# Another distribution of a block's convolution over its sixteen steps

## The chip, the cores and the metric

The kernel runs on one core of a Trainium2 chip. The metric is device time in microseconds of one launch. Engines are named as in the profile: PE (matrix products; PEld are its weight loads), DVE or VectorE, ACT or ScalarE, POOL or GpSimd, SP (which issues the DMA transfers; SPq is its queue).

## The reference

A causal convolution over seven tokens with a softmaxed weight per head, then a two-layer network. All data are float32.

```python
# x: 8 x 4096 x 192, weight: 8 heads x 7 taps; 24 channels share a head
w = softmax(weight, axis=-1)
x_pad = concat([zeros(B, 6, D), x], axis=1)
out[b, s, c] = sum(w[head(c), k] * x_pad[b, s + k, c] for k in range(7))
x = out.reshape(32768, 192)
h = x @ w_in                       # 192 x 2048
g = where(h >= 1, h, where(h <= -1, 0, (h + 1) ** 2 / 4))
return g @ w_out                   # 2048 x 192
```

## The kernel before, in words

The 32768 tokens are 64 tiles of 512; two tiles, A and B, make a block, so there are 32 blocks. Hidden units go in eight pairs of 128, so a tile takes eight steps and a block sixteen. The loop at the end of the kernel runs over steps `q`; `i = q % 16` is the step in the block, and c the block. Steps 0 to 7 are the network on tile A, 8 to 15 on tile B.

To keep float32 precision, matrix operands are split in two parts, hi and lo, and three products are summed. In each step:

- PE runs `mm1(q)` (L422, 18 pairs of products into a PSUM tile `h`, of which there are two) and then `mm2(q - 2)` (L462, 20 into four accumulators: `accm0`, `accm1`, `accr0`, `accr1`), which takes `gh` and `gl` of two steps ago.
- VectorE clips `h` (L473), makes `gl` of the step before (L497, `g - gh`, both from SBUF), and takes the maximum (L484), which frees `h`.
- ScalarE makes `gh` of the step before (L491, a cast), then the square (L479).

After a tile's eighth `mm2`, in steps 1 and 9, ScalarE copies the four accumulators out (L509, four copies), so that the next `mm2` can start; POOL adds them (L511); in steps 2 and 10 follow a small copy (L521) and addition (L522), and VectorE's transposes for the store (L534).

Around this the convolution of the next tokens is done, in channel-major layout. A block has three units: `b` (tile B's first 128 channels, for this same block's steps 8 to 15), `a` (tile A's first 128, for the next block) and `r` (the remaining 64 channels of both tiles, for the next block). A unit goes through:

- "T": VectorE transposes the loaded tile `raw` into `xT` (L147). For `b` this is done at the end of step 15.
- tap 0: ScalarE writes `y = w * xT` (L226). Taps 1 to 6: ScalarE makes a product `p` (L219), POOL adds it to `y` (L230).
- "split": ScalarE casts `y` to hi (L248, for `r` L262); lo is `y - hi`, on POOL for `a` and `b` (L252), on VectorE for `r` (L263). SP issues four transfers that exchange the halves (L235, L236).

Buffers rotate: two each of `xT` and `y`, three of `p`, three of `raw`. All three loads of a block are issued in step 0. Each engine works its instructions in the order in which the program writes them; nothing reorders them. `conv_slot(i, ...)`, called at the end of a step's work on the engines but ahead of the store's part, looks up in three tables, `PLAN_B`, `PLAN_A` and `PLAN_R`, what each unit does in step `i`. Block 0 uses other tables for `a` and `r` (`FIRST_A`, `FIRST_R`).

```python
PLAN_B = {0: (0, 1), 2: (2, 3), 3: (4, 5), 4: (6,), 5: "split"}
PLAN_A = {4: ("T", 0), 5: (1, 2), 6: (3, 4), 7: (5, 6), 8: "split"}
PLAN_R = {7: ("T",), 8: (0, 1, 2), 10: (3, 4), 11: (5, 6), 13: "split"}
```

Of the kernel before, what the change touches and what calls it, by code (L numbers as in the profile page):

```python
# [30 lines left out]
def lightconv_then_ffn(ctx: ExitStack, tc: tile.TileContext, x, weight, w_in, w_out, out):  # L31
# [669 lines left out]

    PLAN_B = {0: (0, 1), 2: (2, 3), 3: (4, 5), 4: (6,), 5: "split"}
    PLAN_A = {4: ("T", 0), 5: (1, 2), 6: (3, 4), 7: (5, 6), 8: "split"}
    PLAN_R = {7: ("T",), 8: (0, 1, 2), 10: (3, 4), 11: (5, 6), 13: "split"}


    FIRST_B = {2: 2, 3: 3, 4: 4, 5: 5}
# [4 lines left out]
    def conv_slot(i, b, a, r):  # L714
        early = b.c == 0
        plans = ((None if early else b, PLAN_B), (a, FIRST_A if early else PLAN_A),
                 (r, FIRST_R if early else PLAN_R))
        for u, plan in plans:
# [201 lines left out]
```

## Time and profile before

| | |
|---|---|
| median of 3 runs | 2170.52 us (2169.75 to 2170.53) |
| profiled execution | 2170.33 us, span 2168.6 us |
| granted PE clock | 0.999 |
| busy | PE 2153.0, DVE 2084.0, ACT 1684.8, POOL 1139.4 us |
| L230, POOL, y + p | 546 x 1454 ns |
| L497, DVE, gl | 497 x 1478 ns |
| L484, DVE, max | 505 x 1215 ns |
| L473, DVE, clip | 505 x 1198 ns |
| L219, ACT, product p | 562 x 714 ns |

Busy shares are averages over the whole run and include the time in which an engine is held up within an instruction. To read where time is lost, follow the start times of the same instruction from step to step. In a row of the timeline the first number is the start in us from the span's start, the second the duration; x6 means six instructions merged in one row, and what stands in brackets is idle time ahead of it and what ended it.

### The profile page before, as it was taken

The numbers are of one execution on the slowest core, as the hardware profiler recorded it, in microseconds if no ns is written. First come the engines' busy times: TensorE is split into PE (matmuls) and PEld (weight loads), VectorE is DVE, ScalarE is ACT, GpSimd is POOL, SyncE is SP. The second block draws the span as 40 slices with busy tenths as digits, with TensorE's granted clock in tenths as the row PEclk, the third lists the DMA queues.
The fourth block names the chain that finished last, engine by engine and source line by source line (L and its number), as shares of the span: only waits on it lengthen the run. The fifth ranks groups of instructions, "written<-read, shape, count | busy, mean of one in ns | idle before, by whom it ended". The sixth has DMA issues, their size and how long they took to land.

```text
span 2168.6 us, 48144 instructions
## 1 busy us (share of the span) xinstructions
PE 2153.0 (99%) x19646; PEld 1875.8 (86%) x19646; DVE 2084.0 (96%) x1883; ACT 1684.8 (78%) x2153; POOL 1139.4 (53%) x868
## 2 busy tenths in 40 slices
PE   9999999999999999999999999999999999999999
PEld 6998888888888888888888888888888888998887
DVE  8899999999999999999999999999999999999998
ACT  7778877778777788777887787877878777788775
POOL 1556644566445565555654456644556545565451
PEclk9999999999999999999999999999999999999999
DMA  6222222222222222222122222222222222212211
GB/s 165 51 53 42 46 50 51 53 51 42 51 48 50 55 41 53 51 48 55 37 51 51 51 53 48 44 49 48 53 55 40 53 51 47 56 35 53 51 35 25
DMA packets 439197, 110.83 MB, mean 51 GB/s; under 512 B 407360, under 2 KB 414912, under 8 KB 438976
## 3 DMA queue, kind: packets, MB, share of 16 engines
q1 hardware_dynamic: 438816, 107.65, 25.9%
q8 instruction: 155, 2.54, 0.5%
q14 instruction: 66, 0.54, 0.1%
q10 hardware_dynamic: 160, 0.10, 0.0%
HBM read 32.84 MB, written 25.17 MB: 27 GB/s over the span
## 4 chain that ended last, share of the span: by engine, by line
DVE 27%; PE 24%; ACT 19%; POOL 13%; issue 13%; SPq 3%; DMA 1%; POOLq 0%; DVEq 0%; ACTq 0%
POOL y L230 11%; PE h L422 10%; DVE g L484 9%; DVE g L473 8%; PE accm L462 7%; DVE gl L497 7%; ACT g L479 6%; ACT gh L491 5%; PE accr L462 4%; ACT t L509 4%; DVE osb L534 2%; SPq L95 2%; ACT p L219 2%; POOL lo L252 2%; DMA raw<-in_x_dram 1%
## 5 line engine op out<-in xcount | busy, mean ns | idle before, releaser
L230 POOL TENSOR_TENSOR y<-y,p 128x512 f32<-128x512 f32 x546 | 793.8, 1454 | 751.0 <-DVE g L484 541.5
L497 DVE TENSOR_TENSOR gl<-g,gh 128x1024 fp32r<-128x1024 f32 (+1 forms) x497 | 734.4, 1478 | 51.6 <-ACT gh L491 41.3
L491 ACT CAST gh<-g 128x1024 fp32r<-128x1024 f32 (+1 forms) x497 | 520.4, 1047 | 255.4 <-DVE g L484 244.1
L422 PE MATMUL h<-hi,w 64*128 64x512 f32 x4032 | 701.2, 377 | 0.0
L479 ACT ACTIVATE g<-g 128x1024 f32<-128x1024 f32 (+1 forms) x505 | 535.1, 1060 | 167.3 <-DVE g L473 157.0
L484 DVE TENSOR_TENSOR g<-h,g 128x1024 f32<-128x1024 f32 (+1 forms) x505 | 613.3, 1215 | 8.3 <-ACT g L479 4.4
L473 DVE TENSOR_SCALAR g<-h 128x1024 f32<-128x1024 f32 (+1 forms) x505 | 604.7, 1198 | 11.6 <-PE h L422 10.6
L462 PE MATMUL accm<-gh,w 64*128 64x512 f32 x3968 | 604.2, 378 | 9.3 <-ACT t L509 9.1
L422 PEld LDWEIGHTS h<-hi,w 64*128 64x128 f32 x4032 | 523.7, 186 | 47.9
L422 PE MATMUL h<-lo,w 64*128 64x512 f32 x2016 | 540.5, 376 | 0.0
L462 PEld LDWEIGHTS accm<-gh,w 64*128 64x128 f32 x3968 | 449.4, 186 | 77.0 <-ACT t L509 29.4
L462 PE MATMUL accm<-gl,w 64*128 64x512 f32 x1984 | 379.2, 381 | 0.0
L219 ACT ACTIVATE p<-xT,wk 128x512 f32<-128x512 f32 x562 | 376.2, 714 | 0.0
L462 PE MATMUL accr<-gh,wr 64*128 64x512 f32 x1984 | 373.4, 376 | 0.0
L462 PE MATMUL accr<-gl,wr 64*128 64x512 f32 x1984 | 373.4, 376 | 0.0
L422 PEld LDWEIGHTS h<-lo,w 64*128 64x128 f32 x2016 | 330.2, 186 | 24.6
L422 PE MATMUL h<-rh,w 64*128 64x512 f32 x992 | 293.5, 376 | 0.0
L422 PE MATMUL h<-rhi,w 64*128 64x512 f32 x992 | 293.5, 376 | 0.0
L462 PEld LDWEIGHTS accm<-gl,w 64*128 64x128 f32 x1984 | 250.9, 186 | 33.4 <-DVE gl L497 12.3
L462 PEld LDWEIGHTS accr<-gl,wr 64*128 64x128 f32 x1984 | 257.3, 186 | 24.8 <-DVE gl L497 0.2
L462 PEld LDWEIGHTS accr<-gh,wr 64*128 64x128 f32 x1984 | 257.3, 186 | 24.7 <-ACT gh L491 0.2
L422 PEld LDWEIGHTS h<-rhi,w 64*128 64x128 f32 x992 | 184.5, 186 | 14.9
(141 smaller groups left out, 1867.6 us busy)
## 6 DMA issues: line engine op xcount, KB each, us to landing
out_dram<-osb SPq DMA_DIRECT2D x366, 64.0 KB
raw<-in_x_dram SPq DMA_DIRECT2D x334, 68.0 KB
hi<-hi SPq DMA_DIRECT2D x126, 128.0 KB
lo<-lo SPq DMA_DIRECT2D x126, 128.0 KB
rhi<-rh SPq DMA_DIRECT2D x62, 128.0 KB
rlo<-rl SPq DMA_DIRECT2D x62, 128.0 KB
words<-in_moe_w_in_dram SPq DMA_DIRECT2D x16, 192.0 KB
words<-in_moe_w_out_dram SPq DMA_DIRECT2D x8, 384.0 KB
```

The costliest lines, as they stand in the source:

```text
L95: (engs[i] if engs else nc.sync).dma_start(out=raw[i * SQ:(i + 1) * SQ, lo:n // SQ + 1, :], in_=src.rearrange("(j a) b -> a j b", a=SQ),)
L219: nc.scalar.mul(p, self.xT[:, SH + k:SH + k + TB], wk[:, self.wsel, k:k + 1])
L230: nc.gpsimd.tensor_add(y, y, self.product(k))
L252: eng.tensor_sub(lo, self.y, hi.bitcast(F32))
L422: nc.tensor.matmul(to, w[HALVES[e], c0:c0 + P], of, start=(n == 0), stop=(n == len(mms) - 1))
L462: nc.tensor.matmul(both(accs[s][a, i]), st, turns(g[HALVES[i], e, :]), start=(j == 0 and n == first[a]), stop=(j == NPAIR - 1 and n == las ...
L473: nc.vector.tensor_scalar(out=g[:, e, :], in0=hs[q][:, e, :], scalar1=-1.0, scalar2=1.0, op0=ALU.max, op1=ALU.min)
L479: nc.scalar.activation(g[:, e, :], g[:, e, :], AF.Square, bias=0.5, scale=0.5)
L484: nc.vector.tensor_tensor(out=g[:, e, :], in0=h[:, e, :], in1=g[:, e, :], op=ALU.max)
L491: nc.scalar.copy(gh[:, e, :], gs[q][:, e, :])
L497: eng.tensor_sub(gl[:, e, :], g[:, e, :], gh[:, e, :])
L509: nc.scalar.copy(t[i][:, n], acc[a, i][:, n])
```

## The change

The three tables are changed; nothing else is.

```diff
-    PLAN_B = {0: (0, 1), 2: (2, 3), 3: (4, 5), 4: (6,), 5: "split"}
-    PLAN_A = {4: ("T", 0), 5: (1, 2), 6: (3, 4), 7: (5, 6), 8: "split"}
-    PLAN_R = {7: ("T",), 8: (0, 1, 2), 10: (3, 4), 11: (5, 6), 13: "split"}
+    PLAN_B = {0: (0, 1, 2), 2: (3, 4), 3: (5, 6), 5: "split"}
+    PLAN_A = {3: ("T", 0), 4: (1, 2), 5: (3, 4), 6: (5, 6), 11: "split"}
+    PLAN_R = {4: ("T",), 7: (0, 1), 8: (2, 3), 10: (4,), 11: (5,), 12: (6,), 13: "split"}
```

Tile B's taps are done by step 3 instead of 4, tile A's begin in step 3 instead of 4 and its split goes from step 8 to 11; the rest's transpose goes from step 7 to 4, and its taps, three, two and two at a time in steps 8, 10 and 11, become two, two, one, one and one in steps 7, 8, 10, 11 and 12.

The order on POOL, one block, before. The first row is the last two additions of the block ahead and this block's first; the two `lo` are B's split and A's.

```order
L230 TENSOR_TENSOR y<-y,p 128x512 x3
L511 TENSOR_TENSOR sum<-t 128x512 x2
L230 TENSOR_TENSOR y<-y,p 128x512 x2
L522 TENSOR_TENSOR sum<-sum,t 64x512
L230 TENSOR_TENSOR y<-y,p 128x512 x3
L252 TENSOR_TENSOR lo_7877<-y,hi_7876 128x512
L230 TENSOR_TENSOR y<-y,p 128x512 x6
L252 TENSOR_TENSOR lo_8049<-y,hi_8048 128x512
L230 TENSOR_TENSOR y<-y,p 128x512 x2
L511 TENSOR_TENSOR sum<-t 128x512 x2
```

The same block on POOL with the change. Here the first row is the last two additions of the block ahead and two of this one.

```order
L230 TENSOR_TENSOR y<-y,p 128x512 x4
L511 TENSOR_TENSOR sum<-t 128x512 x2
L230 TENSOR_TENSOR y<-y,p 128x512 x2
L522 TENSOR_TENSOR sum<-sum,t 64x512
L230 TENSOR_TENSOR y<-y,p 128x512 x4
L252 TENSOR_TENSOR lo_7886<-y,hi_7885 128x512
L230 TENSOR_TENSOR y<-y,p 128x512 x7
L511 TENSOR_TENSOR sum<-t 128x512 x2
L230 TENSOR_TENSOR y<-y,p 128x512
L522 TENSOR_TENSOR sum<-sum,t 64x512
L252 TENSOR_TENSOR lo_8228<-y,hi_8227 128x512
```

One more addition stands ahead of the first sums and one more ahead of B's split; A's `lo` goes behind the second sums (L511). Between the two `lo` stand seven additions, the sums, another addition and L522, where six additions stood.

VectorE, from step 2's gl to step 5's clip, before:

```order
L497 TENSOR_TENSOR gl<-g,gh 128x1024
L484 TENSOR_TENSOR g<-h,g 128x1024
L534 STREAM_TRANSPOSE osb<-sum 128x512
L473 TENSOR_SCALAR g<-h 128x1024
L497 TENSOR_TENSOR gl<-g,gh 128x1024
L484 TENSOR_TENSOR g<-h,g 128x1024
L534 STREAM_TRANSPOSE osb<-sum 64x512
L473 TENSOR_SCALAR g<-h 128x1024
L497 TENSOR_TENSOR gl<-g,gh 128x1024
L484 TENSOR_TENSOR g<-h,g 128x1024
L147 STREAM_TRANSPOSE xT<-raw 128x544
L473 TENSOR_SCALAR g<-h 128x1024
```

The same place with the change, from step 3's clip on:

```order
L473 TENSOR_SCALAR g<-h 128x1024
L497 TENSOR_TENSOR gl<-g,gh 128x1024
L484 TENSOR_TENSOR g<-h,g 128x1024
L147 STREAM_TRANSPOSE xT<-raw 128x544
L534 STREAM_TRANSPOSE osb<-sum 64x512
L473 TENSOR_SCALAR g<-h 128x1024
L497 TENSOR_TENSOR gl<-g,gh 128x1024
L484 TENSOR_TENSOR g<-h,g 128x1024
L147 STREAM_TRANSPOSE xT<-raw 128x544
L473 TENSOR_SCALAR g<-h 128x1024
```

Two unit transposes (A's and the rest's) now stand here instead of one, A's ahead of the store's transpose; the one in step 7 is gone.

ScalarE in steps 8 and 9, up to the copies of the accumulators, before:

```order
L479 ACTIVATE g<-g 128x1024
L248 CAST hi_7127<-y 128x512
L226 ACTIVATE y<-xT,wk 128x512
L219 ACTIVATE p<-xT,wk 128x512 x2
L491 CAST gh<-g 128x1024
L479 ACTIVATE g<-g 128x1024
L509 COPY t<-accm_6750 128x512
```

And with the change:

```order
L479 ACTIVATE g<-g 128x1024
L219 ACTIVATE p<-xT,wk 128x512 x2
L491 CAST gh<-g 128x1024
L479 ACTIVATE g<-g 128x1024
L509 COPY t<-accm_6753 128x512
```

The cast and the tap 0 are gone from between the two squares; two products are left.

## The prediction

> **What bounds the kernel now.** I read the page's busy shares first, then the list of waits, then the start of each step on PE, then VectorE, GpSimd and ScalarE row by row through one block, the fifteenth after the first. All blocks between the second and the last look alike to 0.1 us.
>
> ```profile
> PE 2153.0 (99%) x19646; PEld 1875.8 (86%) x19646; DVE 2084.0 (96%) x1883; ACT 1684.8 (78%) x2153; POOL 1139.4 (53%) x868
> ...
> PEld accm L462 <- ACT t L509: 29.4, 58, 0.7
> DVE gl L497 <- ACT gh L491: 41.3, 110, 0.6
> PEld accm L462 <- DVE gl L497: 12.3, 54, 0.3
> ```
>
> PE and DVE are both nearly full, so averages do not say which one sets the pace. PE waits in two places: for the accumulators to be copied out (58 waits, two in each of 29 blocks) and for gl. The starts of mm1 show where:
>
> ```profile
> 1021.41 0.80 PE L422 MATMUL h<-hi,w 64*128 64x512 f32 x4
> 1025.51 0.80 PE L422 MATMUL h<-hi,w 64*128 64x512 f32 x4
> ...
> 1046.01 0.80 PE L422 MATMUL h<-hi,w 64*128 64x512 f32 x4
> 1050.33 0.60 PE L422 MATMUL h<-hi,w 64*128 64x512 f32 x4
> ...
> 1058.54 0.59 PE L422 MATMUL h<-hi,w 64*128 64x512 f32 x4
> 1062.79 0.59 PE L422 MATMUL h<-hi,w 64*128 64x512 f32 x4
> 1067.75 0.80 PE L422 MATMUL h<-hi,w 64*128 64x512 f32 x4
> ...
> 1088.26 0.80 PE L422 MATMUL h<-hi,w 64*128 64x512 f32 x4
> ```
>
> These are steps 0, 1, 6, 7, 9, 10, 11 of one block and step 0 of the next. An undisturbed step is 4.10 us, sixteen are 65.62 (the five steps from 1025.51 to 1046.01 are 20.50). The block takes 66.85. The 1.23 us lie in step 6 (4.32 instead of 4.10), step 9 (4.25) and step 10 (4.96). If nothing held PE, 29 blocks would be 35.7 us shorter.
>
> **What makes PE wait** is the chain on VectorE. Per step it runs clip (L473), gl of the step before (L497), max (L484); max to max is the length of a step there.
>
> ```profile
> 1027.00 1.23 DVE L484 TENSOR_TENSOR g<-h,g 128x1024 f32<-128x1024 f32 x1
> ...
> 1029.39 1.31 DVE L497 TENSOR_TENSOR gl<-g,gh 128x1024 fp32r<-128x1024 f32 x1
> 1030.63 1.21 DVE L484 TENSOR_TENSOR g<-h,g 128x1024 f32<-128x1024 f32 x1
> ...
> 1035.09 1.21 DVE L484 TENSOR_TENSOR g<-h,g 128x1024 f32<-128x1024 f32 x1
> ...
> 1037.95 2.11 DVE L497 TENSOR_TENSOR gl<-g,gh 128x1024 fp32r<-128x1024 f32 x1
> 1039.99 1.21 DVE L484 TENSOR_TENSOR g<-h,g 128x1024 f32<-128x1024 f32 x1
> ...
> 1044.06 1.22 DVE L484 TENSOR_TENSOR g<-h,g 128x1024 f32<-128x1024 f32 x1
> 1045.20 0.73 DVE L147 STREAM_TRANSPOSE xT<-raw 128x544 f32<-128x544 f32 x1
> ...
> 1047.66 1.22 DVE L497 TENSOR_TENSOR gl<-g,gh 128x1024 fp32r<-128x1024 f32 x1 [0.62 <-ACT gh L491]
> 1048.80 1.22 DVE L484 TENSOR_TENSOR g<-h,g 128x1024 f32<-128x1024 f32 x1
> ...
> 1056.30 1.21 DVE L484 TENSOR_TENSOR g<-h,g 128x1024 f32<-128x1024 f32 x1
> ...
> 1059.20 2.13 DVE L497 TENSOR_TENSOR gl<-g,gh 128x1024 fp32r<-128x1024 f32 x1
> 1061.26 1.21 DVE L484 TENSOR_TENSOR g<-h,g 128x1024 f32<-128x1024 f32 x1
> ...
> 1064.86 1.22 DVE L484 TENSOR_TENSOR g<-h,g 128x1024 f32<-128x1024 f32 x1
> ...
> 1069.57 1.21 DVE L484 TENSOR_TENSOR g<-h,g 128x1024 f32<-128x1024 f32 x1
> ...
> 1074.39 1.21 DVE L484 TENSOR_TENSOR g<-h,g 128x1024 f32<-128x1024 f32 x1
> ...
> 1081.99 1.22 DVE L484 TENSOR_TENSOR g<-h,g 128x1024 f32<-128x1024 f32 x1
> ...
> 1093.85 1.23 DVE L484 TENSOR_TENSOR g<-h,g 128x1024 f32<-128x1024 f32 x1
> ```
>
> The maxes are those of steps 0, 1, 2, 3, 4, 5, 7, 8, 9, 10, 11, 13 and the next block's 0: 66.85 in all. A step in which nothing is in the way is 3.60 (1061.26 to 1064.86), and gl is ready 2.4 after the max (1027.00 to 1029.39). Longer steps have two causes, seen on the other two engines:
>
> ```profile
> 1028.34 1.29 POOL L230 TENSOR_TENSOR y<-y,p 128x512 f32<-128x512 f32 x1 [17.80 <-DVE g L484]
> ...
> 1037.71 1.27 POOL L522 TENSOR_TENSOR sum<-sum,t 64x512 f32<-64x512 f32 x1
> ...
> 1050.41 9.84 POOL L230 TENSOR_TENSOR y<-y,p 128x512 f32<-128x512 f32 x6
> ```
> ```profile
> 1027.48 0.71 ACT L219 ACTIVATE p<-xT,wk 128x512 f32<-128x512 f32 x1
> ...
> 1045.96 0.73 ACT L226 ACTIVATE y<-xT,wk 128x512 f32<-128x512 f32 x1 [1.32 <-DVE xT L147]
> ...
> 1061.43 1.32 ACT L219 ACTIVATE p<-xT,wk 128x512 f32<-128x512 f32 x2
> ...
> 1064.59 1.06 ACT L509 COPY t<-accm 128x512 f32<-128x512 f32 x2
> ```
>
> First, a gl that becomes ready during a GpSimd addition waits for its end. At 1059.20 the last of the six additions runs until 1060.25, and gl ends at 1061.33, 1.08 later, instead of taking 1.22; at 1037.95 the addition of L522 ends at 1038.98 and gl at 1040.06, again 1.08. The six additions, 1.29 each alone, need 9.84 because they wait for gl in turn. Second, ScalarE works in order: the y of tap 0 waits for the transpose (1.32 idle), gh stands behind it, gl comes 0.62 late, and that is PE's stall in step 6. The stall in step 10 is the copy-out that only starts at 1064.59.
>
> **The change.** No instruction is added or removed; each moved one has its old price, and only its place counts. I carry the chain from max to max with four prices from the rows above: a product 0.66 on ScalarE, an addition starting 0.15 after its product (1028.19 to 1028.34), 1.29 for it plus 0.08 to the next, and 1.08 for a gl behind it, with the next max 0.07 ahead of gl's end (1061.33 to 1061.26). A step with two products right behind its square thus has its additions from 0.7 to 3.36 after max, and is 4.37 long; with one addition, over at 2.0, it is 3.60; with y and two products it is 5.0.
>
> - Step 0, B's taps 0 to 2 in place of 0 and 1: 3.63 becomes 5.0. The second addition starts only 0.08 ahead of gl; the other order makes step 0 3.9 and step 2 later by 0.3 to 0.5.
> - Step 1, copy-out: 4.46 becomes 3.5. The copies move back only 0.25 (behind the third product), while max moves back 1.4, so gh and the next gl no longer wait for them.
> - Step 2, three GpSimd additions as before: 4.90 becomes 4.40, since gl now meets the second tap's addition near its end and goes ahead of L522's.
> - Step 3, A's transpose and tap 0 come here: 4.07 becomes 4.95. The transpose (0.66) stands ahead of the store's; y waits for it and gh for y; gl then still meets B's last addition for 0.3.
> - Step 4, A's taps 1 and 2 and the rest's transpose: 4.74 becomes 4.25. No y holds gh any more (0.62 gone); two additions come, and the transpose lies within the wait for them.
> - Steps 5 and 6: 7.50 (1048.80 to 1056.30) becomes 7.7; the same kinds of work with the additions about 0.3 later.
> - Step 7: 4.96 becomes 3.6. Its transpose (0.66) is gone, and one addition instead of two ends ahead of or just with gl.
> - Step 8, no split, two products, no y: 3.60 becomes 4.3.
> - Step 9, copy-out: 4.71 becomes 3.8. ScalarE reaches it at 1063.9 instead of 1064.59 and the GpSimd sums are done that much sooner.
> - Step 10, one tap instead of two: 4.82 becomes 4.1. Steps 11 and 12 (1074.39 to 1081.99, 7.60): 7.7 with A's split and single taps. From 1081.99 to 1093.85 nothing moves: 11.86.
>
> The gains in steps 1, 2, 4, 7, 9, 10 are 4.84, the losses in 0, 3, 5 to 6, 8, 11 to 12 are 3.35. The chain falls from 66.85 to 65.36. That is below PE's 65.62, so PE would set the pace, with VectorE drifting ahead of it by up to 0.5 until a clip waits for mm1 at the end of a block.
>
> Is each gl in time for PE then? PE wants gl of step i about 2.80 after mm1 of step i+2 starts: with undisturbed steps at 1044.7 (gl of 3), 1048.8 (4) and 1052.9 (5). Without any drift the chain delivers at 44.96, 49.21, 53.34, up to 0.43 late; with 0.5 drift all are early, the worst by 0.1. The copies of step 9 are done by 1064.4 and 1064.9, minus the drift, against a need of 1064.4 and 1064.6: no stall. The three thin places I charge 0.05 us a block.
>
> Two moves at nothing. A's four exchange transfers go three steps later on SP's queue, past the four stores of step 10 and ahead of the two of step 11. By one row,
> ```profile
> 1071.43 6.21 SPq L538 DMA_DIRECT2D out_dram<-osb  x6
> ```
> these take about 1.03 each, so the transfers are issued by 1077, ten us before the next block's mm1. A's raw tile is loaded in step 0, far ahead of step 3. If that cover went, mm1 of step 0 would wait once per block.
>
> Sum: the profiled execution is 2170.33 (span 2168.6, median of the runs 2170.52). Less 29 x 1.23 = 35.7, plus 29 x 0.05 = 1.5: **2136**.
>
> **Rivals.**
> - Half the gain. The drift does not build up because some step is 0.3 longer than I worked out; the gl of steps 3 to 5 then hold PE 0.43 a block. Gain 29 x 0.8 = 23: 2147. For it: the margins of 0.1. Against: the chain needs only 65.36.
> - gl costs its full 1.22 behind an addition, 0.14 more in each meeting. I count 12 meetings a block in the new order and 8 now, so the new chain is 65.36 + 4 x 0.14 = 65.92, the gain 29 x 0.93 = 27: 2143. Against it: the two rows with 1.08. The Trainium skill ("SBUF — State Buffer", section "Who interferes with whom") says that a VectorE instruction with two SBUF inputs and a GpSimd one that reads SBUF exclude each other, and that the loser blocks for the whole of the other. The waits above agree with that; the 0.14 is what rows have and the rule does not, and by the rule alone the time is this rival's.
> - No change: GpSimd is still at A's additions in step 7 and gl meets two there. Step 7 stays at 4.9 and the chain at 66.7: 2166 to 2170.
> - Slower. Steps 3 and 4 have gl meeting the last 0.33 of an addition. If the additions run 0.96 later there (the third POOL operation of step 2 is in front of them), both wait for a whole 1.29: 1.9 more, chain 67.3, 29 x 0.43 = 12.5 on top: 2183. It decides once the extra waits pass 1.49. For it: 16 POOL operations in steps 0 to 6 instead of 14. Against: the additions cannot start later than their products plus one gl.
>
> **How the numbers follow.** Forecast 0.60 (own range 2131 to 2142), whole-length gl 0.10, half 0.15, none 0.06, slower 0.09. About 4 us, 0.2%, is what a measurement can tell from no change. Faster 0.85, same 0.06, slower 0.09. The low end is PE never waiting, 2134, less 3 for prices I rounded up; the high end takes in half the gain and some of its error, 2155.
>
> **What would show it.** PE's mm1 at 4.10 throughout, above all from step 9 to 11 (9.21 now, 8.2 then); PEld's waits for t (29.4) near zero; step 0 on VectorE 5.0 and step 7 3.6; the 1.32 idle before y moved to step 3; POOL without a break in steps 2 to 6. The prediction is wrong if gl of steps 3 to 5 becomes what PE waits for, or if VectorE's block stays above 66.

## The result, and the profile after

The changed kernel takes 2134.30 us (median, 2134.03 to 2134.82) against 2170.31 us, a ratio of 0.9835 with a 95% interval of 0.982 to 0.9849: 36 us, 1.65%, less. The profiled execution is 2134.82 us, its span 2133.1.

The page's first part, and the engine shares of the chain that ended last:

```profile
span 2133.1 us, 48144 instructions
...
PE 2127.3 (100%) x19646; PEld 2071.4 (97%) x19646; DVE 2056.3 (96%) x1883; ACT 1697.2 (80%) x2153; POOL 1120.9 (53%) x868
...
PE 100%; ACT 0%; DVE 0%; issue 0%; POOL 0%; POOLq 0%; ACTq 0%
```

The chain that ended last lies wholly on PE now; before, VectorE had 27% of it, PE 24%, ScalarE 19%. From the list of waits (engine, what it waited for, us in total, times, longest):

```profile
DVE g L473 <- PE h L422: 38.0, 101, 1.6
...
DVE gl L497 <- ACT gh L491: 9.1, 32, 0.6
```

PE's waits for the copies `t` (29.4 before) and for `gl` (12.3) no longer appear. Instead VectorE's clip waits for PE: 38.0 us against 10.6. PE's starts of mm1 in the fifteenth block, steps 0, 1, 9, 10, 11 and the next step 0:

```profile
1006.27 0.78 PE L422 MATMUL h<-hi,w 64*128 64x512 f32 x4
1010.37 0.78 PE L422 MATMUL h<-hi,w 64*128 64x512 f32 x4
...
1043.18 0.78 PE L422 MATMUL h<-hi,w 64*128 64x512 f32 x4
1047.28 0.78 PE L422 MATMUL h<-hi,w 64*128 64x512 f32 x4
1051.38 0.78 PE L422 MATMUL h<-hi,w 64*128 64x512 f32 x4
...
1071.89 0.78 PE L422 MATMUL h<-hi,w 64*128 64x512 f32 x4
```

Every step is 4.10. Steps 9 and 10 together are 8.20 (9.21 before), the block 65.62 (66.85 before). 29 blocks at 1.23 are 35.7; the two profiled spans differ by 35.5. The whole gain is PE's three stalls, gone in every block. The maxes on VectorE, steps 0 to 5, 7 to 11, 13, 15 and the next 0:

```profile
1011.08 1.23 DVE L484 TENSOR_TENSOR g<-h,g 128x1024 f32<-128x1024 f32 x1
...
1016.07 1.21 DVE L484 TENSOR_TENSOR g<-h,g 128x1024 f32<-128x1024 f32 x1
...
1019.65 1.21 DVE L484 TENSOR_TENSOR g<-h,g 128x1024 f32<-128x1024 f32 x1
...
1023.97 1.21 DVE L484 TENSOR_TENSOR g<-h,g 128x1024 f32<-128x1024 f32 x1
...
1028.81 1.21 DVE L484 TENSOR_TENSOR g<-h,g 128x1024 f32<-128x1024 f32 x1
...
1032.97 1.21 DVE L484 TENSOR_TENSOR g<-h,g 128x1024 f32<-128x1024 f32 x1
...
1040.60 1.21 DVE L484 TENSOR_TENSOR g<-h,g 128x1024 f32<-128x1024 f32 x1
1044.12 1.23 DVE L484 TENSOR_TENSOR g<-h,g 128x1024 f32<-128x1024 f32 x1
1048.49 1.21 DVE L484 TENSOR_TENSOR g<-h,g 128x1024 f32<-128x1024 f32 x1
1052.45 1.21 DVE L484 TENSOR_TENSOR g<-h,g 128x1024 f32<-128x1024 f32 x1
1056.52 1.23 DVE L484 TENSOR_TENSOR g<-h,g 128x1024 f32<-128x1024 f32 x1
...
1064.32 1.23 DVE L484 TENSOR_TENSOR g<-h,g 128x1024 f32<-128x1024 f32 x1
...
1072.53 1.23 DVE L484 TENSOR_TENSOR g<-h,g 128x1024 f32<-128x1024 f32 x1
1076.70 1.23 DVE L484 TENSOR_TENSOR g<-h,g 128x1024 f32<-128x1024 f32 x1
```

Differences of these rows against those of before, in us:

| step | 0 | 1 | 2 | 3 | 4 | 5, 6 | 7 | 8 | 9 | 10 | 11, 12 | 13 to 15 |
|---|---|---|---|---|---|---|---|---|---|---|---|---|
| before | 3.63 | 4.46 | 4.90 | 4.07 | 4.74 | 7.50 | 4.96 | 3.60 | 4.71 | 4.82 | 7.60 | 11.86 |
| worked out | 5.0 | 3.5 | 4.40 | 4.95 | 4.25 | 7.7 | 3.6 | 4.3 | 3.8 | 4.1 | 7.7 | 11.86 |
| after | 4.99 | 3.58 | 4.32 | 4.84 | 4.16 | 7.63 | 3.52 | 4.37 | 3.96 | 4.07 | 7.80 | 12.38 |

The columns are max to max on VectorE. Steps 13 to 15 are longer because clip now waits for mm1 there. Steps 0 to 3 together cost VectorE 0.67 more than before and step 8 another 0.77; steps 4, 7, 9 and 10 give back 3.52.

### The profile page after: what moved, and what is told of

Same layout as the page of the kernel before. It is cut to its first block, busy times and chain, and to the rows that moved or that the text cites. A ratio compares the mean times of both kernels' runs of the same rounds, so it can differ in the third digit from the quotient of the medians.

```text
span 2133.1 us, 48144 instructions
## 1 busy us (share of the span) xinstructions
PE 2127.3 (100%) x19646; PEld 2071.4 (97%) x19646; DVE 2056.3 (96%) x1883; ACT 1697.2 (80%) x2153; POOL 1120.9 (53%) x868
## 4 chain that ended last, share of the span: by engine, by line
PE 100%; ACT 0%; DVE 0%; issue 0%; POOL 0%; POOLq 0%; ACTq 0%
PE h L422 47%; PE accm L462 30%; PE accr L462 20%; PE accr L440 1%; PE accm L440 1%; PE accr L190 0%; PE accm L609 0%; PE accr L422 0%; PE h L564 0%; PE accm L181 0%; PE accr L564 0%; PE h L155 0%; DVE t L558 0%; PE accr L653 0%; ACT xT L168 0%
## 5 line engine op out<-in xcount | busy, mean ns | idle before, releaser
L230 POOL TENSOR_TENSOR y<-y,p 128x512 f32<-128x512 f32 x546 | 753.2, 1382 | 730.1 <-ACT p L219 711.0
L497 DVE TENSOR_TENSOR gl<-g,gh 128x1024 fp32r<-128x1024 f32 (+1 forms) x497 | 701.1, 1411 | 12.7 <-ACT gh L491 9.1
L422 PEld LDWEIGHTS h<-hi,w 64*128 64x128 f32 x4032 | 587.8, 186 | 8.0
L422 PE MATMUL h<-lo,w 64*128 64x512 f32 x2016 | 570.8, 376 | 0.0
L462 PEld LDWEIGHTS accm<-gh,w 64*128 64x128 f32 x3968 | 499.9, 186 | 7.9
L422 PEld LDWEIGHTS h<-lo,w 64*128 64x128 f32 x2016 | 374.7, 186 | 4.6 <-DMA lo<-lo 0.5
L462 PEld LDWEIGHTS accr<-gh,wr 64*128 64x128 f32 x1984 | 289.6, 186 | 4.0
L462 PEld LDWEIGHTS accm<-gl,w 64*128 64x128 f32 x1984 | 289.6, 186 | 4.0
L462 PEld LDWEIGHTS accr<-gl,wr 64*128 64x128 f32 x1984 | 289.5, 186 | 4.0
L511 POOL TENSOR_TENSOR sum<-t 128x512 f32<-128x512 f32 (+1 forms) x124 | 155.9, 1280 | 95.3 <-ACT t L509 70.6
```

The source lines that it names most:

```text
L230: nc.gpsimd.tensor_add(y, y, self.product(k))
L422: nc.tensor.matmul(to, w[HALVES[e], c0:c0 + P], of, start=(n == 0), stop=(n == len(mms) - 1))
L462: nc.tensor.matmul(both(accs[s][a, i]), st, turns(g[HALVES[i], e, :]), start=(j == 0 and n == first[a]), stop=(j == NPAIR - 1 and n == las ...
L497: eng.tensor_sub(gl[:, e, :], g[:, e, :], gh[:, e, :])
L511: nc.gpsimd.tensor_add(y[:, n], t[0][:, n], t[1][:, n])
```

## Experiments: what bounds the block, and by how much

Theory: VectorE's chain, lengthened where gl meets a GpSimd addition or waits for gh, must stay under PE's 65.62 a block. First rival: only ScalarE's queue ahead of the copies (step 8) matters, GpSimd does not. All times are medians; each stands beside runs of the kernel before on the same chip (2169.9 to 2170.3).

**No additions.** In the kernel before:

```diff
-                    nc.gpsimd.tensor_add(y, y, self.product(k))
+                    self.product(k)
```

> The kernel before without GpSimd's additions of taps 1 to 6 from block 1 on (each y stays tap 0 alone); ScalarE still makes every product. Chain: gl meets only sums and lo, the block falls under PE's 65.6: 2133 to 2137. Copies: ScalarE's queue is unchanged, the copies stay late: 2165 to 2171.

Measured: 2134.66 (ratio 0.9836, 0.9819 to 0.9852). Its page:

```profile
PE 2127.2 (100%) x19646; PEld 1880.7 (88%) x19646; DVE 2003.7 (94%) x1883; ACT 1687.4 (79%) x2153; POOL 343.5 (16%) x322
```

This kernel leaves the additions out of its result; ScalarE has all its instructions, and PE is at its bound all the same. In the kernel before, ScalarE's list of waits names a GpSimd instruction once in the whole run (0.7), so the additions reach the copies through VectorE. The first rival falls: the copies were late because VectorE's chain was late, not because of ScalarE's queue alone.

**Added VectorE work in the changed kernel**, one and two more transposes of the same tile at the end of step 15:

```diff
             conv_n["b"].transpose()
+            for _ in range(2):        # 1 in the other run
+                nc.vector.transpose(out=conv_n["b"].xT, in_=conv_n["b"].raw.rearrange("p j b -> p (j b)"))
```

> The changed kernel with B's transpose done twice at the end of step 15 (0.66 us more on VectorE per block, same data). Chain: about 0.6 of slack a block is left (clips wait 0.16 and 0.41 for PE in steps 9 and 15), so this just fits: 2134 to 2140. If the chain's slack is only the 0.26 that the prediction worked out: 65.36 + 0.66 = 66.02, 2146. If VectorE were far from bounding: 2134.

> The same with two extra transposes (1.32 us more per block). Chain with 0.6 slack: 66.3 a block, 2150 to 2158. With 0.26 slack: 2165. If VectorE were far from bounding: 2134.

Measured: 2138.01 with one, 2161.09 with two. The first lies in the range for 0.6 of slack, the second 3 us above it. The max of step 15 and the next block's first, with two:

```profile
1084.00 1.23 DVE L484 TENSOR_TENSOR g<-h,g 128x1024 f32<-128x1024 f32 x1
...
1089.73 1.22 DVE L484 TENSOR_TENSOR g<-h,g 128x1024 f32<-128x1024 f32 x1
```

5.73 instead of 4.17: each extra transpose costs 0.78, not the 0.66 I had taken. The block that ends here is 66.54 with both, so without them the chain is at most 66.54 - 1.56 = 64.98, 0.6 under PE. With one it is then 64.98 + 0.78 = 65.76, 0.14 over PE or about 4 us in 29 blocks, and the run with one took 3.7 us more than the changed kernel. This is the room that the change made: 66.85 to 65.0, of which PE can use 1.23.

## Experiments: which part of the change does it

**B's plan alone**, in the kernel before:

```diff
-    PLAN_B = {0: (0, 1), 2: (2, 3), 3: (4, 5), 4: (6,), 5: "split"}
+    PLAN_B = {0: (0, 1, 2), 2: (3, 4), 3: (5, 6), 5: "split"}
```

> The kernel before with B's new plan alone (taps 0 to 2 in step 0, done by step 3). Chain: step 0 1.4 longer, steps 1 and 2 1.4 shorter together, the late gh of step 4 stays: 2165 to 2173. Copies: nothing changes in steps 8 and 9: 2170.

Measured: 2170.54, no change (1.0001, 0.9992 to 1.0011). Steps 0 to 2 became 4.99, 3.52 and 4.39, as worked out for them: lost and won back within three steps. Both theories had this value.

**The rest's plan alone, the rest's old plan in the changed kernel, A's split moved alone, A's split left in step 8:**

```diff
# rest_alone: the kernel before, with
+    PLAN_R = {4: ("T",), 7: (0, 1), 8: (2, 3), 10: (4,), 11: (5,), 12: (6,), 13: "split"}
# rest_old: the changed kernel, with
+    PLAN_R = {7: ("T",), 8: (0, 1, 2), 10: (3, 4), 11: (5, 6), 13: "split"}
# split_11_alone: the kernel before, with
+    PLAN_A = {4: ("T", 0), 5: (1, 2), 6: (3, 4), 7: (5, 6), 11: "split"}
# split_8: the changed kernel, with
+    PLAN_A = {3: ("T", 0), 4: (1, 2), 5: (3, 4), 6: (5, 6), 8: "split"}
```

> The kernel before with the new plan of the rest unit alone. Chain: GpSimd is still at A's taps 5 and 6 in step 7, the rest's tap 1 queues behind them, A's split and two taps pile up in step 8, so nothing is gained there; about 0.6 us a block longer: 2172 to 2190. Copies: ScalarE's step 8 loses y, 0.6 us a block earlier copies: about 2152.

> The changed kernel with the old plan of the rest unit (transpose in step 7, taps 0 to 2 in step 8, two taps in steps 10 and 11); B's and A's new plans stay. Theory of the chain (VectorE's max-to-max chain, lengthened by meetings of gl with GpSimd additions and by late gh, must stay under PE's 65.6 us a block): step 7 gets its 0.66 transpose back, step 8 has y and two products (5.0 instead of 4.4), step 10 two taps, step 11 A's split and two taps; about 2 us more than the changed kernel's chain, so about 67 a block: 2165 to 2190. Theory of the copies (only ScalarE's work in step 8, ahead of the accumulator copies, counted; GpSimd does not matter): A's cast is gone from step 8, 0.5 us less there than in the kernel before, so about 2155.

> The kernel before with A's split moved to step 11 and nothing else. Chain: step 8's gl now meets the additions of the rest's taps (0.6 longer), step 10 no better, step 11 0.3 longer; no gain: 2166 to 2178. Copies: ScalarE's step 8 loses 0.5 us, the copies come 0.5 earlier and PE's stall in step 10 falls from 0.86 to 0.35: about 2155.

> The changed kernel with A's split back in step 8. Chain: in step 8 the two products' additions already hold gl to 4.4 us, the lo ahead of them fits before gl, step 11 becomes lighter; PE stays the bound: 2134 to 2138. Copies: ScalarE's step 8 gets 0.5 us back, copies 0.5 later, of which the changed kernel has 0.37 to spare: up to 4 us more, 2134 to 2138; if the copies had no slack, about 2148.

Two combinations were added to fill the table: the kernel before with A's split in step 11 and the rest's new plan (split_11_rest), and the changed kernel with the split in step 8 and the rest's old plan (early_split_8).

> The kernel before with A's split in step 11 and the rest's new plan; A's and B's taps stay as they were. Chain: step 7 stays near 4.9 (the additions of A's last taps and the rest's first queue there), steps 8 to 10 as light as in the changed kernel: about 65.6 to 66.0 a block, 2134 to 2148. If each part adds its own gain (29 us for the split, 7 us lost for the rest): 2148.

> The changed kernel's plans of B and A, with A's split in step 8 and the rest's old plan. ScalarE has hi, y and two products in step 8 again, so gh and the copies come late: about 66.5 a block, 2150 to 2170. If taps that are done sooner are what helps: 2134 to 2140.

| A's and B's taps | the rest's plan | A's split in step 8 | A's split in step 11 |
|---|---|---|---|
| old | old | 2170 (before) | 2141.05 |
| old | new | 2177.13 | 2146.21 |
| new | old | 2149.43 | 2148.58 |
| new | new | 2134.62 | 2134.30 (the change) |

Two of my numbers missed widely: the split alone (2166 to 2178 expected, 2141 measured) and the rest's old plan (2165 to 2190 expected, 2149 measured). The rest's plan alone, split_8 and split_11_rest lie in their ranges, early_split_8 0.6 us below its own; the range of split_11_rest held the value of adding the parts, too, so this run does not tell the two apart. In the first miss I had forecast no saving in step 10 and had no term for steps 9 and 2; the next section measures savings in all three. In the second I had about 67 a block and it is 66.1: steps 5 and 9 came out at 3.53 each, against 4.04 and 3.96 in the changed kernel. So the chain carried by hand, which was close for the change itself, was off by 25 us and 16 us here. The theory of the copies was off by 25 us for the rest's plan alone, 14 for the split alone and 6 for the rest's old plan. The table says:

- The parts do not add. Moving the split alone brings 29 us, but with the other two parts in place it brings nothing (2134.62 and 2134.30), since PE's bound is already reached.
- The rest's new plan costs 5 to 7 us with the old taps and brings 14 to 15 with the new ones. What it was to gain it does not gain with the old taps: its first taps come in step 7, and A's last two are there too, so ScalarE has three products and a tap 0 ahead of gh. The run with the rest's plan alone shows it in its timeline:

```profile
1059.97 1.32 ACT L219 ACTIVATE p<-xT,wk 128x512 f32<-128x512 f32 x2
1061.19 0.71 ACT L226 ACTIVATE y<-xT,wk 128x512 f32<-128x512 f32 x1
1061.80 0.71 ACT L219 ACTIVATE p<-xT,wk 128x512 f32<-128x512 f32 x1
1062.42 1.03 ACT L491 CAST gh<-g 128x1024 fp32r<-128x1024 f32 x1
```
```profile
1063.48 1.76 DVE L497 TENSOR_TENSOR gl<-g,gh 128x1024 fp32r<-128x1024 f32 x1 [0.93 <-ACT gh L491]
```

gl waits 0.93 for gh, so step 7 stays at 4.95 although its transpose is gone. With A's taps a step sooner, step 7 is 3.52. The loss itself lies in steps 4 and 5, where the rest's transpose now stands behind A's: 4.79 and 4.09 instead of 4.74 and 3.91, which is 0.23 a block or 6.7 us in 29 blocks.

## Experiments: which half of the split

Its 29 us could come from GpSimd's `lo` or from ScalarE's cast leaving step 8. One run moves only `lo` (the kernel before, `PLAN_A` with `8: "hi", 11: "lo"`), the other moves the split but gives ScalarE the load back (`PLAN_R` with `8: (0, 0, 1, 2)`, tap 0 written twice).

> The kernel before, of A's split only the GpSimd half (lo and its transfers) moved from step 8 to 11; ScalarE's cast hi stays in step 8. It asks which half of the split's move brought the 29 us of the split moved alone (2141). If GpSimd's place in step 8 counts: 2139 to 2145. If it is ScalarE's cast ahead of y, the two products and gh in step 8: 2165 to 2175 (the second addition then catches gl in step 8, which costs what the lo freed).

> The kernel before with A's whole split moved to step 11, and ScalarE's tap 0 of the rest (0.62 us) written twice in step 8, so that ScalarE has the old load there without the split. If ScalarE's load in step 8 counts: the 29 us are gone again, 2165 to 2175. If GpSimd's lo counts: 2139 to 2145.

Measured: 2140.77 with `lo` alone moved, 2174.55 with ScalarE's load given back. The two contradict each other if one half alone is to be the cause. The steps (differences of the maxes) resolve most of it:

| | step 2 | 8 | 9 | 10 | 11 | 8 to 11 |
|---|---|---|---|---|---|---|
| before | 4.90 | 3.60 | 4.71 | 4.82 | 4.06 | 17.19 |
| split in 11 | 4.07 | 4.06 | 3.94 | 4.07 | 4.64 | 16.71 |
| lo alone in 11 | 4.08 | 4.61 | 3.52 | 4.38 | 4.18 | 16.69 |
| split in 11, tap 0 twice | 4.91 | 4.81 | 3.47 | 4.38 | 4.72 | 17.38 |

In steps 8 to 11 the move is worth only 0.5, with the cast or without: one `lo` less in step 8 saves 0.6 in steps 8 to 10 and costs 0.1 in step 11; the cast saves another 0.45 and costs the same in step 11. The larger piece, 0.83, is in step 2, where nothing was moved. The run with `lo` alone moved, VectorE and then GpSimd:

```profile
1024.48 1.18 DVE L473 TENSOR_SCALAR g<-h 128x1024 f32<-128x1024 f32 x1
1025.59 1.20 DVE L497 TENSOR_TENSOR gl<-g,gh 128x1024 fp32r<-128x1024 f32 x1
```
```profile
1023.01 2.65 POOL L230 TENSOR_TENSOR y<-y,p 128x512 f32<-128x512 f32 x2 [1.29 <-ACT p L219]
1025.62 2.31 POOL L522 TENSOR_TENSOR sum<-sum,t 64x512 f32<-64x512 f32 x1
```

gl starts at 1025.59, the two additions end at 1025.66, and L522's addition waits for gl (2.31 long). In the kernel before, L522's addition started at 1037.71, 0.24 ahead of gl, and gl took 2.11. Which of the two comes first turns on a quarter of a microsecond. One block of the kernel before, with nothing changed, has the other order:

```profile
905.00 1.20 DVE L497 TENSOR_TENSOR gl<-g,gh 128x1024 fp32r<-128x1024 f32 x1
906.20 1.22 DVE L484 TENSOR_TENSOR g<-h,g 128x1024 f32<-128x1024 f32 x1
```
```profile
905.01 2.33 POOL L522 TENSOR_TENSOR sum<-sum,t 64x512 f32<-64x512 f32 x1
```

Its step 2 is 4.07 and the block 66.09, where its neighbours have 4.90 and 66.86. In the run with `lo` alone moved, one block has L522's addition at 432.33, 0.03 ahead of gl; its step 2 is 5.13 and the block 66.58 instead of 65.78. So the order by itself is worth about 0.8 a block. In the two runs with 2141 us the rows suggest why it comes out well in nearly every block: where VectorE enters the block 0.5 earlier against PE, step 2's clip waits longer for mm1 (0.47 instead of 0.12), the square and the two products come later relative to gl, and gl goes first. The three runs with the old taps and their additions whose chain fell (split in 11, `lo` alone, split with the rest's new plan) show 4.07 or 4.08 there; those that did not gain (before, the rest's plan alone, tap 0 twice) show 4.90 to 4.93. That the half microsecond saved in steps 8 to 11 is what turns the order is argued from these rows; no run of its own forces it. The changed kernel has gl ahead of L522's addition in step 2, too, as the prediction counted on, but its third tap makes step 0 longer: steps 0 to 2 are 4.99, 3.58 and 4.32, together 12.89 against 12.99, so it gains almost nothing there.

## Why the prediction was right

- The bound: PE at 4.10 a step with three stalls caused by VectorE's chain. Shown by the run without additions and by the two doses. The time by itself says little of the rest: any chain under 65.62 a block gives the same 2134 us, so the chain is tested by its steps and by the doses.
- The four prices carried from row to row. Up to step 12 they were within 0.17 step by step (table above). The sum in the prediction has a slip: its own steps gain 4.94 and lose 3.25, not 4.84 and 3.35, so they make 65.16 a block and not 65.36. It did not show in the time, since both lie under 65.62. Up to step 12 they add up to 53.30, and 53.24 was measured; the doses put the whole chain at 65.0 or less. With the right sum the rival by which gl needs its full 1.22 would have come to 65.72 and about 2138, too near the forecast for the time to tell; there are also 10 meetings in the new order, not 12. Its rows decide. The addition in step 0 did start just ahead of gl, and gl then ended 1.09 after it, so that rival falls:

```profile
1012.41 2.65 POOL L230 TENSOR_TENSOR y<-y,p 128x512 f32<-128x512 f32 x2 [14.97 <-ACT p L219]
```
```profile
1013.86 2.29 DVE L497 TENSOR_TENSOR gl<-g,gh 128x1024 fp32r<-128x1024 f32 x1
```

The additions end at 1015.06, gl at 1016.15. The Trainium skill ("SBUF — State Buffer", section "Who interferes with whom") has the loser blocked for the whole of the other's instruction; the trace agrees, except that gl ends 1.09 after the addition and not its full 1.22.

- The drift. I allowed 0.5 and charged 1.5 us for thin places. The max of step 0 now starts 4.81 after its mm1 instead of 5.59, a drift of 0.8. The gl with the least room (step 4) ends at 1033.05, 0.6 before PE's first product with it:

```profile
1031.71 1.34 DVE L497 TENSOR_TENSOR gl<-g,gh 128x1024 fp32r<-128x1024 f32 x1
```
```profile
1033.68 0.78 PE L462 MATMUL accm<-gl,w 64*128 64x512 f32 x4
```

So the rival of half the gain falls, and the charge was the mis-sized term: 35.5 us gained between the profiled executions, 34.2 forecast.

- The copies of step 9. They start at 1047.79, 4.61 after mm1 of that step, against 6.05 before; the first is done at 1048.36, 0.86 before PE's first product into that accumulator. No stall in step 10, as forecast.

```profile
1047.79 1.05 ACT L509 COPY t<-accm 128x512 f32<-128x512 f32 x2
```
```profile
1049.22 1.21 PE L462 MATMUL accm<-gh,w 64*128 64x512 f32 x8
```

- What was taken at nothing. A's exchange transfers went out from 1057.40 to 1059.84, between the stores of steps 10 and 11; in the whole list of waits PE waits for an exchanged `lo` once, 0.5.
- Two readings that did not hold. GpSimd was to run without a break in steps 2 to 6, and it has two breaks of 1.5 there (ahead of 1029.32 and 1033.47), waiting for ScalarE. And the blocks of the kernel before are not all alike to 0.1: one is 67.15, and the one of 66.09 shown above held the clue that an order can flip.
- What the prediction did not see: that smaller edits would have done most of it (the split's move alone, 29 us) or all of it (the earlier taps with the rest's new plan but the split left alone). It credited each step with its saving and added them up, and the eight combinations show that the parts of the change cannot be added: past PE's bound a saving is worth nothing, and short of it a change of order can add to one.

None of the kernels tried beats the changed one. With every step at PE's 4.10, another order of the convolution has nothing left to win in these 29 blocks.

## What to carry to other kernels

When two engines are both at 96% or more, find which start times repeat at a constant step and where they slip, then carry the other engine's chain by hand from one fixed instruction to the next: four measured prices were enough to forecast a gain of 1.6% here. Mark each place where two instructions come within a quarter of a microsecond of each other: the same method was off by 25 us for the split alone, where one such order flipped. In a step with a fixed window, count what one in-order engine must do before the next link of the chain (here two products fit between a square and gh, while three and a tap 0 made gl wait 0.93), and spread small work so that no step goes over. Judge a part of a plan together with the others, since past the bound it shows nothing.

## What the runs showed of the hardware that was not expected

- A GpSimd addition and VectorE's two-input subtraction exclude each other in the order of arrival, also between queued additions. Two additions into the same `y` leave a gap of about 0.08 (1.37 from start to start, 1.29 long), and a gl that waits at that time goes first: in the kernel before, gl of 1051.30 ends at 1052.79, and the addition that starts at 1051.78 takes 2.15. Between an addition and L522's there is no such gap in the rows; L522's above was held because gl had started 0.03 sooner.
- An addition that starts 0.24 ahead of gl costs VectorE 0.9; one that starts 0.03 behind costs it nothing.
- A second transpose of the same tile, right behind the first, adds 0.78 to VectorE's step, where a transpose followed by clip took 0.66. It is the same tile that matters: in the run with the rest's plan alone two transposes into different tiles stand one behind the other in step 4, and they take 1.28 up to the clip, 0.64 each.
